# Retention, then a routed expert layer, then a squared-ReLU MLP: state products in four quarter tiles, first queries by blocks, later expert weights, other banks

## The chip, the cores and the metric

One Trainium2 core runs the whole program in one launch. The metric is the device time of one execution in microseconds. Before the change three executions took 484.52, 486.38 and 487.38 us; the median is 486.38 us.

## The reference

Three layers run one after the other, all in float32.

1. Retention. For each of 2 sequences and 8 heads (768 positions, head size 64), `state = gamma_h * state + outer(k_t, v_t)` and `y_t = q_t @ state / 8`. The heads' rows of 64 numbers side by side make 1536 tokens of 512 numbers.
2. Routed experts. `logits = x @ w_gate` for 8 experts; each token goes to its best expert, to the next free place there (384 places at most, in order of the tokens), through `relu(x @ w1[e]) @ w2[e]` (512 to 1024 to 512), and is scaled by its softmax weight. Tokens without a place give zero.
3. MLP: `relu(x @ w_in)**2 @ w_out`, 512 to 2048 to 512.

```python
state = gamma[None, :, None, None] * state + np.einsum('bhd,bhe->bhde', k[:, :, t], v[:, :, t])
y[:, :, t] = scale * np.einsum('bhd,bhde->bhe', q[:, :, t], state)
```

## The kernel before

Tokens are worked through in 12 tiles of 128 (6 for each sequence), the loop over `i` at L564, one turn for each tile. The order of every engine's queue is the order of the program, written out by hand (`manual_schedule`), so an instruction that waits holds up all behind it on its engine. TensorE is PE, VectorE DVE, ScalarE ACT, GpSimd POOL; SP issues nearly all DMAs.

Powers of gamma are folded into the rows of q and k: `khat` (L347, POOL) and `qhat` (L351, POOL) multiply, `ktrans` and `qtrans` (L360, L367) transpose four pairs of heads on PE and copy out of PSUM on ACT. Queries are loaded for two tiles at a time (L339, 512 KB). Tile `i` then needs three products. `scores` (L385) makes k times q for both heads of each of the 4 pairs, and DVE masks it into `A`. `outer` (L399) adds k times v to the running state in bank `pp`, and ACT copies it to `TF`. `attend` (L413) writes `xo`, transposed (features by tokens): the state's part at L423 (`TF` by the queries, float32, 64 rows by 64 columns of the array), then the part of the tile's own values at L426 (128 rows by 64 columns). At L423 head 0 of a pair uses rows 0 to 63 and columns 0 to 63, head 1 the other rows and the other columns, all into the one bank `xo`.

`halve` (L430) splits `xo` into two float16 halves, `xhi` on ACT and `xlo` on DVE. `gate` (L440) takes the logits from them in bank `lg`; `natural` (L471) transposes both back into bank `xn`, ACT copies them to `row`, and SP writes `row` to HBM. `probs`, `count`, `rank` (L497), `spread` and `enter` (L510) work out expert, weight and place; `rank` and `enter` use bank `lg` too. The eight PSUM banks are tk, tq, sc0, sc1, pp, xo, lg, xn, one tile in each.

Beside this the turns prepare the first expert's weights: 1 MB loads, their number capped by turn (L567), and splits into float16 halves, `split_hi` on ACT and `split_lo` on DVE (`half_step`, L268). From turn 3 on (`PRE`, L520) each turn has about one of each. The last two tiles are handled apart: turn 10 gathers the rows of expert 0 that are known (L582), runs `attend` of tile 11 inside the same turn (L598) and leaves the loop; L617 to L655 then add the last two tiles to expert 0's input through `p0` and the products into `xb` (L529, L634). The experts' layer starts behind it (L706) and PE is busy without a break from there to the end.

Of the kernel before, what the change touches and what calls it, by code (L numbers as in the profile page):

```python
# [27 lines left out]
def layout_consts(B, H, S, D, E, cap, widths):  # L28
# [9 lines left out]
    cols["gq"] = (gamma[None, None, :, None] ** (tq - S // 2) * 4.0).reshape(P, -1)  # L38
    cols["mask"] = (t[:, None] <= t[None, :]).astype(np.float64)
# [22 lines left out]
def kernel(  # L62
# [263 lines left out]

    Q, K, V = {}, {}, {}
# [3 lines left out]
    def load(i):  # L331
        b, c = divmod(i, NC)
        todo = [(K, k, "k")] + ([(Q, q, "q")] if c % 2 == 0 else []) + [(V, v, "v")]
        if i == 0:
            todo[0], todo[1] = todo[1], todo[0]
        for store, src, nm in todo:
            if store is Q:
                Q[i // 2] = ld.tile([P, H, 2, D], F32, name=nm, tag=nm, bufs=2)
                nc.sync.dma_start(Q[i // 2], src[b, :, c * P:(c + 2) * P, :].rearrange("h (p r) d -> p h r d", r=2))  # L339
            else:  # L340
                store[i] = ld.tile([P, H, D], F32, name=nm, tag=nm)
# [3 lines left out]
    HALF = [slice(j * D, (j + 1) * D) for j in range(2)]  # L345
# [5 lines left out]
    def qhat(u, r, eng=POOL):  # L351
        if 2 * u >= NT:
            return
        QH[u, r] = sb.tile([P, H, D], F32, name="qh", tag="qh")
        eng.tensor_tensor(QH[u, r], Q[u][:, :, r, :],
# [4 lines left out]
    def ktrans(i):  # L360
# [4 lines left out]
        ACT.activation(out=KT[i], in_=tk, func=AF.Copy)  # L365

    def qtrans(u, r, tag="tq", eng=ACT):  # L367
# [8 lines left out]
        o, x = QT[u][:, :, :, :, r], tq.rearrange("p n (c i) -> p n c i", c=2)  # L376
        if eng is DVE:
            DVE.tensor_copy(out=o, in_=x)
        else:
            ACT.activation(out=o, in_=x, func=AF.Copy)  # L380
# [32 lines left out]
    def attend(i):  # L413
        b, c = divmod(i, NC)
        xo = ps.tile([P, NP, P], F32, name="xo", tag="xo")
# [4 lines left out]
        if c:  # L420
            for p in range(NP):
                for r in HALF:
                    PE.matmul(xo[r, p, :], lhsT=TF[i][r, p, :], rhs=qt[r, p, :], start=(p == 0), stop=False, skip_group_check=True)  # L423
        for p in range(NP):
            for j, r in enumerate(HALF):
                PE.matmul(xo[r, p, :], lhsT=vv[:, 2 * p + j, :], rhs=a[:, j, p, :],  # L426
                          start=(c == 0 and p == 0), stop=(p == NP - 1), skip_group_check=True)
        XO[i] = xo

    def halve(i):  # L430
        xo = XO.pop(i)
# [39 lines left out]
    def natural(i, apart=False):  # L471
# [6 lines left out]
        if not apart:  # L478
            ACT.activation(out=row, in_=xn.rearrange("p s k t -> p s (k t)"), func=AF.Copy)
# [40 lines left out]
    PRE = 8  # L520
# [43 lines left out]
    for i in range(L):  # L564
        if i + LA < NT:
            load(i + LA)
        state["cap"] = min((i + 1) // 2 if i < 8 else i - 2, 4 * FIXED - 1)  # L567
        do_loads()
        if i == 5:
            clear()  # L570
# [44 lines left out]
        if L - PRE <= i and (i + 1) % NC:  # L615
            half_step(split_lo)
# [624 lines left out]
```

## Time and profile before

| | us |
|---|---|
| three executions | 484.52, 486.38, 487.38 |
| the profiled execution | 485.2 |
| its span, first to last instruction | 483.4 |
| attention's first product of tile 0's values (L426) | at 13.34 |
| experts' first product (L706) | at 87.15 |

An instruction's row gives its start, its duration, engine, line and the tiles it writes and reads; `x16` means that sixteen like it were merged. A float32 product on PE appears as two instructions. In brackets stands how long the engine idled before it, and for whom. A matmul's own duration (about 270 ns) overlaps with its neighbours'; what a group costs is the time from its start to the next group's start.

### The profile page before, as it was taken

How to read it: one execution, taken by the hardware profiler on the slowest of the kernel's cores; microseconds unless marked ns; L12 is line 12 of the kernel's file. 1: busy time of each engine (PE TensorE's matmuls, PEld its weight loads, DVE VectorE, ACT ScalarE, POOL GpSimd, SP SyncE). 2: the span in 40 equal slices, each digit the busy share in tenths (PEclk: the TensorE clock that was granted, in tenths of full speed). 3: DMA queues.
4: the chain of work that ended last, by engine and by line, in shares of the span. 5: the costliest groups of instructions: out<-in, count | busy, mean ns of one | idle time of the engine just before them, and what ended most of it. 6: DMA issues, size and time to landing. Idle time of an engine off the chain costs nothing.

```text
span 483.4 us, 10140 instructions
## 1 busy us (share of the span) xinstructions
PE 464.8 (96%) x4229; PEld 351.1 (73%) x4229; DVE 316.5 (65%) x552; ACT 265.3 (55%) x396; POOL 81.4 (17%) x99
## 2 busy tenths in 40 slices
PE   7999898999999999999999999999999999999994
PEld 4788787999999999999744444444458884447883
DVE  2457678898978879887699999407673114666111
ACT  2456666677667668663266666339882006885010
POOL 1544332542032131211200000020000110000001
PEclk8899999999999999999999999999999999999998
DMA  9999994799999979887443000011000100000001
GB/s 195 240 274 259 283 345 143 276 397 353 128 344 329 280 260 364 240 306 254 91 172 91 0 1 0 1 43 43 2 1 1 45 23 22 1 0 1 23 24 49
DMA packets 56120, 71.35 MB, mean 148 GB/s; under 512 B 30705, under 2 KB 37233, under 8 KB 55042
## 3 DMA queue, kind: packets, MB, share of 16 engines
q1 hardware_dynamic: 53410, 63.77, 43.9%
q0 software_dynamic: 2512, 6.73, 3.8%
q8 instruction: 35, 0.57, 0.5%
q10 hardware_dynamic: 144, 0.11, 0.2%
q14 instruction: 19, 0.16, 0.1%
HBM read 63.77 MB, written 6.84 MB: 146 GB/s over the span
## 4 chain that ended last, share of the span: by engine, by line
PE 81%; DVE 7%; DMA 4%; issue 3%; ACT 3%; POOL 1%; SPq 0%; POOLq 0%; ACTq 0%; DVEq 0%
PE w L1071 14%; PE zp L900 9%; PE zp L901 9%; PE zp L899 9%; PE yp L723 4%; PE yp L724 4%; PE yp L722 4%; PE hp L706 4%; PE hp L708 4%; PE hp L707 4%; PE op L925 3%; PE op L924 3%; PE op L923 3%; PE xo L426 2%; DMA gx<-xd,gidx 2%
## 5 line engine op out<-in xcount | busy, mean ns | idle before, releaser
L899 PE MATMUL zp<-yhi,winhi 128*128 128x512 f16 x192 | 72.8, 379 | 0.0
L901 PE MATMUL zp<-yhi,winlo 128*128 128x512 f16 x192 | 72.8, 379 | 0.0
L900 PE MATMUL zp<-ylo,winhi 128*128 128x512 f16 x192 | 72.8, 379 | 0.0
L723 PE MATMUL yp<-hl,w2hi 128*128 128x232 f16 (+5 forms) x256 | 65.5, 256 | 0.4 <-DVE hl L712 0.4
L722 PE MATMUL yp<-hh,w2hi 128*128 128x232 f16 (+5 forms) x256 | 65.5, 256 | 0.0
L724 PE MATMUL yp<-hh,w2lo 128*128 128x232 f16 (+5 forms) x256 | 65.5, 256 | 0.0
L1071 PE MATMUL w<-WH,AH 128*128 128x256 f16 x224 | 61.1, 273 | 0.5 <-ACT ob L1086 0.5
L1071 PE MATMUL w<-WL,AH 128*128 128x256 f16 x224 | 61.1, 273 | 0.0
L1071 PE MATMUL w<-WH,AL 128*128 128x256 f16 x224 | 61.1, 273 | 0.0
L706 PE MATMUL hp<-xg,w1hi 128*128 128x192 f16 (+5 forms) x224 | 57.1, 255 | 0.0
L708 PE MATMUL hp<-xg,w1lo 128*128 128x192 f16 (+5 forms) x224 | 57.1, 255 | 0.0
L707 PE MATMUL hp<-xg,w1hi 128*128 128x192 f16 (+5 forms) x224 | 57.0, 255 | 0.0
L914 POOL DMA_INDIRECT out_dram<-ob,tid x12 | 11.8, 982 | 224.2 <-DVE ob L1092 124.9
L1071 PEld LDWEIGHTS <-AH 128*128 128x128 f16 x448 | 43.8, 98 | 6.4 <-issue 0.9
L151 DVE SCALAR_TENSOR_TENSOR w2lo<-raw,w2hi 128x1024 f16<-128x1024 f32 x32 | 39.8, 1247 | 8.3 <-ACT w2hi L148 8.3
L1039 DVE TENSOR_TENSOR AL<-x,AH 128x768 f16<-128x768 f32 (+1 forms) x32 | 34.8, 1087 | 15.0 <-ACT AH L1037 15.0
L151 DVE SCALAR_TENSOR_TENSOR w1lo<-raw,w1hi 128x1024 f16<-128x1024 f32 x32 | 39.6, 1244 | 1.2 <-ACT w1hi L148 1.2
L900 PEld LDWEIGHTS <-winhi 128*128 128x128 f16 x192 | 18.8, 98 | 22.5 <-DVE ylo L729 0.2
L901 PEld LDWEIGHTS <-winlo 128*128 128x128 f16 x192 | 18.8, 98 | 22.6
L899 PEld LDWEIGHTS <-winhi 128*128 128x128 f16 x192 | 18.8, 98 | 22.5
L286 POOL DMA_INDIRECT gx<-xd,gidx x16 | 19.7, 1231 | 82.3 <-PE xt L689 72.3
L148 ACT ACTIVATE w2hi<-raw 128x1024 f16<-128x1024 f32 x32 | 33.4, 1051 | 0.0
(180 smaller groups left out, 995.7 us busy)
## 6 DMA issues: line engine op xcount, KB each, us to landing
raw<-in_moe_w_dram SPq DMA_DIRECT2D x32, 1024.0 KB, 7.3
rawi<-in_moe_w_in_dram SPq DMA_DIRECT2D x8, 1024.0 KB, 8.4
rawo<-in_moe_w_out_dram SPq DMA_DIRECT2D x8, 1024.0 KB, 7.0
q<-in_q_dram SPq DMA_DIRECT2D x6, 512.0 KB, 6.7
k<-in_k_dram SPq DMA_DIRECT2D x12, 256.0 KB, 4.5
v<-in_v_dram SPq DMA_DIRECT2D x12, 256.0 KB, 5.8
xd<-row SPq DMA_DIRECT2D x12, 256.0 KB, 4.0
xd<-zrow SPq DMA_DIRECT2D x2, 256.0 KB, 7.8
```

What stands on the lines that cost most here:

```text
L151: DVE.scalar_tensor_tensor(out=lo, in0=raw, scalar=WS, in1=hi, op0=ALU.mult, op1=ALU.subtract)
L706: PE.matmul(o, lhsT=w1h[:, kk, c], rhs=xh[kk], start=(kk == 0), stop=False)
L707: PE.matmul(o, lhsT=w1h[:, kk, c], rhs=xl[kk], start=False, stop=False)
L708: PE.matmul(o, lhsT=w1l[:, kk, c], rhs=xh[kk], start=False, stop=(kk == KD - 1))
L722: PE.matmul(o, lhsT=w2h[:, kk, c], rhs=hh[:, kk, :], start=(kk == 0), stop=False)
L723: PE.matmul(o, lhsT=w2h[:, kk, c], rhs=hl[:, kk, :], start=False, stop=False)
L724: PE.matmul(o, lhsT=w2l[:, kk, c], rhs=hh[:, kk, :], start=False, stop=(kk == KF - 1))
L899: PE.matmul(zp, lhsT=winhi[:, kk, c], rhs=yhi[kk // 2][:, kk % 2, cc], start=(kk == 0), stop=False)
L900: PE.matmul(zp, lhsT=winhi[:, kk, c], rhs=ylo[kk // 2][:, kk % 2, cc], start=False, stop=False)
L901: PE.matmul(zp, lhsT=winlo[:, kk, c], rhs=yhi[kk // 2][:, kk % 2, cc], start=False, stop=(kk == KD - 1))
L1039: DVE.tensor_tensor(AL[:, s, p, :], x[p][:, s, :], AH[:, s, p, :], op=ALU.subtract)
L1071: PE.matmul(o, lhsT=a[:, s, kk, c], rhs=b[:, kk, w, :], start=(start and n == 1), stop=(stop and n == end), skip_group_check=True)
```

## The change

- `attend` writes two PSUM tiles of half the size, `xo[0]` in bank `xo` (pairs 0 and 2) and `xo[1]` in bank `xn` (pairs 1 and 3). In the odd pairs the two heads change places in the output: rows 0 to 63 of the array go to columns 64 to 127, and the other way round. So the features of odd pairs lie swapped; `w_gate` is loaded with the same swap by four DMAs in place of one, `halve` works in two pieces, and `natural` swaps back with three ACT copies in place of one.
- The queries of tiles 0 and 1 are loaded as two blocks of 128 tokens (256 KB each), not as interleaved pairs; later query loads come one turn earlier. Buffers: q 3, k 3, v 5.
- The start is reordered: `khat(0)` and the copy of `ktrans(0)` go to DVE, `qhat(0, 1)` to POOL, and `scores(0)` stands before the second block's transposes.
- The loads of the experts' weights are capped lower in each turn, and the splits begin in turn 5 in place of 3. Turn 9 ends with two low splits in place of one, and turn 10 has one more high and low split, between `rank` and the end of the loop. By the experts' start the same nine have been made. The zeroing of the last rows moves from turn 5 to turn 7.
- `rank` uses bank `sc0` and `enter` bank `tk` for all but the last tiles, so `lg` holds logits alone.

```diff
     def later_consts():
         nc.sync.dma_start(c16, c16_d)
-        nc.sync.dma_start(wg, w_gate.rearrange("(k p) e -> p k e", p=P))
+        wgd = w_gate.rearrange("(k u j p) e -> u j p k e", u=2, j=2, p=D)
+        for u in range(2):
+            for j, r in enumerate(HALF):
+                nc.sync.dma_start(wg[r, u::2, :], wgd[u, j ^ u])
...
     def attend(i):
-        xo = ps.tile([P, NP, P], F32, name="xo", tag="xo")
+        xo = [ps.tile([P, NP // 2, P], F32, name="xo", tag=t) for t in ("xo", "xn")]
...
-                for r in HALF:
-                    PE.matmul(xo[r, p, :], lhsT=TF[i][r, p, :], rhs=qt[r, p, :], start=(p == 0), ...
+                for j, r in enumerate(HALF):
+                    PE.matmul(xo[p % 2][HALF[j ^ p % 2], p // 2, :], lhsT=TF[i][r, p, :], rhs=qt[r, p, :], start=(p < 2), ...
...
     def halve(i):
-        ACT.activation(out=xhi, in_=xo, func=AF.Copy, scale=XS)
-        DVE.scalar_tensor_tensor(out=xlo, in0=xo, scalar=XS, in1=xhi, op0=ALU.mult, op1=ALU.subtract)
+        for u, xo in enumerate(XO.pop(i)):
+            ACT.activation(out=xhi[:, u::2, :], in_=xo, func=AF.Copy, scale=XS)
+            DVE.scalar_tensor_tensor(out=xlo[:, u::2, :], in0=xo, scalar=XS, in1=xhi[:, u::2, :], op0=ALU.mult, op1=ALU.subtract)
...
     natural:
-            ACT.activation(out=row, in_=xn.rearrange("p s k t -> p s (k t)"), func=AF.Copy)
+            ACT.activation(out=o[:, :, :, 0], in_=x[:, :, :, 0], func=AF.Copy)
+            for j in range(2):
+                ACT.activation(out=o[:, :, :, 1, j], in_=x[:, :, :, 1, 1 - j], func=AF.Copy)
...
-        rk = ps.tile([P, E], F32, name="rk", tag="lg" if i < L - 1 else "pp")
+        rk = ps.tile([P, E], F32, name="rk", tag="sc0" if i < L - 1 else "pp")
-        tb_ = ps.tile([P, NB, E], F32, name="tb", tag="lg" if i < L - 1 else "pp" if i < L else "xn")
+        tb_ = ps.tile([P, NB, E], F32, name="tb", tag="tk" if i < L - 1 else "pp" if i < L else "xn")
...
-    PRE = 8
+    PRE = 6
...
-    qhat(0, 1, DVE)
-    khat(0, POOL)
+    khat(0, DVE)
     qtrans(0, 0)
-    qtrans(0, 1, "sc1", DVE)
-    ktrans(0)
+    ktrans(0, DVE)
+    qhat(0, 1, POOL)
+    scores(0)
     khat(1, POOL)
-    scores(0)
+    qtrans(0, 1)
+    outer(0)
     ktrans(1)
-    outer(0)
...
-        state["cap"] = min((i + 1) // 2 if i < 8 else i - 2, 4 * FIXED - 1)
+        state["cap"] = max(0, i - 1) // 2 if i < 8 else i - 3
-        if i == 5:
+        if i == 7:
             clear()
...
             attend(L)
             half_step(split_lo)
             rank(i)
+            half_step(split_hi)
+            half_step(split_lo)
             break
...
         if L - PRE <= i and (i + 1) % NC:
+            half_step(split_lo)
+        if i == L - 2:
+            half_step(split_hi)
             half_step(split_lo)
```

## Rows read from the trace of the kernel before

**Rows 1.** The page: busy time by engine, and PE in 40 slices of 12.1 us.
```profile
PE 464.8 (96%) x4229; PEld 351.1 (73%) x4229; DVE 316.5 (65%) x552; ACT 265.3 (55%) x396; POOL 81.4 (17%) x99
...
PE   7999898999999999999999999999999999999994
```

**Rows 2.** Busy time in four stretches: turns 1, 6, 7 and the tail.
```profile
20.35:26.48 6.13, 5.87 (x99) 5.21 (x97) 3.06 (x12) 2.79 (x7) 2.66 (x5) 1.00 0.99 221
...
51.17:57.41 6.24, 5.02 (x85) 4.36 (x82) 4.45 (x13) 4.16 (x10) 2.16 (x4) 1.00 1.02 326
57.41:63.60 6.19, 5.88 (x100) 5.21 (x98) 4.20 (x13) 4.16 (x10) 2.64 (x5) 1.00 1.00 250
...
80.16:87.15 6.99, 5.96 (x97) 5.33 (x96) 5.61 (x26) 4.80 (x10) 2.38 (x6) 1.00 0.42 129
```

**Rows 3.** The chain that ended last, in order of time, through turn 7.
```profile
57.48 1.02 PE xo L423 x16
58.50 1.05 PE xo L426 x16
...
59.63 0.61 ACT xhi L434
...
60.26 0.69 DVE xlo L435
60.95 0.10 DVE table L516
...
62.00 0.61 PE pp L408 x16
...
63.20 0.44 PE tq L375 x4
```

**Rows 4.** Waits in turns 0 to 10: total us, times, longest.
```profile
PE lg L444 <- DVE table L516: 2.8, 9, 0.3
...
PE rk L500 <- ACT pr L462: 1.6, 3, 0.9
```

**Rows 5.** Timeline of POOL in turns 0 and 1.
```profile
14.61 2.05 POOL L355 TENSOR_TENSOR qh<-q,c 128x512 f32<-128x512 f32 x2 [0.89 <-DMA q<-in_q_dram]
...
22.52 1.05 POOL L355 TENSOR_TENSOR qh<-q,c 128x512 f32<-128x512 f32 x1 [2.53 <-PE xo L426]
23.52 1.04 POOL L349 TENSOR_TENSOR kh<-k,c 128x512 f32<-128x512 f32 x1
```

**Rows 6.** Two stretches of the start: busy times, granted clock, DMA share, GB/s.
```profile
8.00:12.00 4.00, 3.31 (x23) 2.70 (x24) 0.80 (x2) 0.60 (x1) 1.04 (x1) 0.53 1.21 221
12.00:16.00 4.00, 4.00 (x49) 3.37 (x49) 1.06 (x4) 1.70 (x4) 2.44 (x3) 0.62 1.28 253
```

**Rows 7.** Timeline of turns 7 and 8: ACT copies and DVE splits.
```profile
57.13 0.37 ACT L411 ACTIVATE tf<-pp 128x256 f32<-128x256 f32 x1
...
57.95 1.22 DVE L151 SCALAR_TENSOR_TENSOR w1lo<-raw,w1hi 128x1024 f16<-128x1024 f32 x1
...
62.08 1.02 ACT L479 ACTIVATE row<-xn 128x1024 f16<-128x1024 f16 x1 [0.92 <-ACT w2hi L148]
...
64.41 2.06 DVE L151 SCALAR_TENSOR_TENSOR w2lo<-raw,w2hi 128x1024 f16<-128x1024 f32 x1
```

**Rows 8.** Timeline of the tail.
```profile
80.16 1.09 PE L423 MATMUL xo<-qt,tf 64*64 64x128 f32 x16
80.32 1.02 ACT L479 ACTIVATE row<-xn 128x1024 f16<-128x1024 f16 x1 [0.64 <-ACT w2hi L148]
...
82.73 0.34 DVE L526 TENSOR_SCALAR p<-c,rnk,oh 128x232 f16<-128x232 f16 x1
...
83.12 0.95 PE L532 MATMUL xb<-p,row 128*128 128x232 f16 x8 [0.70 <-DVE p L526]
```

**Rows 9.** SP's issue of the gate's weights, in the timeline.
```profile
7.82 0.43 SPq L310 DMA_DIRECT2D wg<-in_moe_w_gate_dram  x1
```

**Rows 10.** The page: the weights' loads, KB each, us from issue to landing.
```profile
raw<-in_moe_w_dram SPq DMA_DIRECT2D x32, 1024.0 KB, 7.3
```

More of the change, by code (lines that the diff above doesn't have):

```diff
@@ L325 @@
     R = [cst.tile([P, E], F16, name=f"R{i}") for i in range(2)]
+    HALF = [slice(j * D, (j + 1) * D) for j in range(2)]
     Q, K, V = {}, {}, {}
@@ L332, in load @@
         b, c = divmod(i, NC)
-        todo = [(K, k, "k")] + ([(Q, q, "q")] if c % 2 == 0 else []) + [(V, v, "v")]
-        if i == 0:
-            todo[0], todo[1] = todo[1], todo[0]
+        u = i // 2 if i in (2, 4) else (i + 1) // 2 if i > 4 and i % 2 else NT
+        todo = [(K, k, "k")] + ([(Q, q, "q")] if 2 * u < NT else []) + [(V, v, "v")]
+        if i < 2:
+            todo = [(Q, q, "q"), (K, k, "k"), (V, v, "v")]
         for store, src, nm in todo:
-            if store is Q:
-                Q[i // 2] = ld.tile([P, H, 2, D], F32, name=nm, tag=nm, bufs=2)
-                nc.sync.dma_start(Q[i // 2], src[b, :, c * P:(c + 2) * P, :].rearrange("h (p r) d -> p h r d", r=2))
+            if store is Q and i < 2:
+                if i == 0:
+                    both = ld.tile([P, 2, H, D], F32, name=nm, tag=nm, bufs=3)
+                    Q[0, 0], Q[0, 1] = both[:, 0], both[:, 1]
+                nc.sync.dma_start(Q[0, i], src[b, :, c * P:(c + 1) * P, :].rearrange("h t d -> t h d"))
+            elif store is Q:
+                Q[u] = ld.tile([P, H, 2, D], F32, name=nm, tag=nm, bufs=3)
+                bq, cq = divmod(2 * u, NC)
+                nc.sync.dma_start(Q[u], src[bq, :, cq * P:(cq + 2) * P, :].rearrange("h (p r) d -> p h r d", r=2))
             else:
-                store[i] = ld.tile([P, H, D], F32, name=nm, tag=nm)
+                store[i] = ld.tile([P, H, D], F32, name=nm, tag=nm, bufs=3 if store is K else 5)
                 nc.sync.dma_start(store[i], src[b, :, c * P:(c + 1) * P, :].rearrange("h t d -> t h d"))
     QH, KH, KT, QT, A = {}, {}, {}, {}, {}
-    HALF = [slice(j * D, (j + 1) * D) for j in range(2)]
     def khat(i, eng=POOL):
@@ L358, in qhat, with ktrans @@
             Q.pop(u)
-    def ktrans(i):
+    def ktrans(i, eng=ACT):
         tk = ps.tile([P, NP, P], F32, name="tk", tag="tk")
@@ L364, in ktrans @@
         KT[i] = sb.tile([P, NP, P], F32, name="kt", tag="kt")
-        ACT.activation(out=KT[i], in_=tk, func=AF.Copy)
+        if eng is DVE:
+            DVE.tensor_copy(out=KT[i], in_=tk)
+        else:
+            ACT.activation(out=KT[i], in_=tk, func=AF.Copy)
     def qtrans(u, r, tag="tq", eng=ACT):
@@ L376, in qtrans @@
         o, x = QT[u][:, :, :, :, r], tq.rearrange("p n (c i) -> p n c i", c=2)
+        if u == 0:
+            o, x = QT[u][:, :, r].rearrange("p n i r -> p n (i r)"), tq
         if eng is DVE:
@@ L421, in attend @@
             for p in range(NP):
-                for r in HALF:
-                    PE.matmul(xo[r, p, :], lhsT=TF[i][r, p, :], rhs=qt[r, p, :], start=(p == 0), stop=False, skip_group_check=True)
+                for j, r in enumerate(HALF):
+                    PE.matmul(xo[p % 2][HALF[j ^ p % 2], p // 2, :], lhsT=TF[i][r, p, :], rhs=qt[r, p, :], start=(p < 2), stop=False,
+                              skip_group_check=True)
         for p in range(NP):
-            for j, r in enumerate(HALF):
-                PE.matmul(xo[r, p, :], lhsT=vv[:, 2 * p + j, :], rhs=a[:, j, p, :],
-                          start=(c == 0 and p == 0), stop=(p == NP - 1), skip_group_check=True)
+            for j in range(2):
+                PE.matmul(xo[p % 2][HALF[j ^ p % 2], p // 2, :], lhsT=vv[:, 2 * p + j, :], rhs=a[:, j, p, :],
+                          start=(c == 0 and p < 2), stop=(p >= NP - 2), skip_group_check=True)
         XO[i] = xo
     def halve(i):
-        xo = XO.pop(i)
         xhi = sb.tile([P, KD, P], F16, name="xhi", tag="xhi")
         xlo = sb.tile([P, KD, P], F16, name="xlo", tag="xlo")
-        ACT.activation(out=xhi, in_=xo, func=AF.Copy, scale=XS)
-        DVE.scalar_tensor_tensor(out=xlo, in0=xo, scalar=XS, in1=xhi, op0=ALU.mult, op1=ALU.subtract)
+        for u, xo in enumerate(XO.pop(i)):
+            ACT.activation(out=xhi[:, u::2, :], in_=xo, func=AF.Copy, scale=XS)
+            DVE.scalar_tensor_tensor(out=xlo[:, u::2, :], in0=xo, scalar=XS, in1=xhi[:, u::2, :], op0=ALU.mult, op1=ALU.subtract)
         XT[i] = (xhi, xlo)
@@ L478, in natural @@
         if not apart:
-            ACT.activation(out=row, in_=xn.rearrange("p s k t -> p s (k t)"), func=AF.Copy)
+            o, x = [y.rearrange("p s (k u) (j d) -> p s k u j d", u=2, j=2) for y in (row.rearrange("p s (k t) -> p s k t", k=KD), xn)]
+            ACT.activation(out=o[:, :, :, 0], in_=x[:, :, :, 0], func=AF.Copy)
+            for j in range(2):
+                ACT.activation(out=o[:, :, :, 1, j], in_=x[:, :, :, 1, 1 - j], func=AF.Copy)
         else:
```

5 lines of the change are left out of this document (added).

## Prediction

> **What bounds the kernel now.** I read the page first: PE is busy for 96% of the span, and the slices show where it is not: in the first seven, the attention [rows 1]. From the experts' first product at 87.15 us to the end PE has no break, and the change touches nothing there, so its whole worth is how much earlier that product starts. The stretches by turn come next: turns 1 to 9 take 6.12 to 6.24 us each, with PE busy for 5.9 of it in turns 1 and 7 and 5.0 in turn 6, and the other engines well below [rows 2]. So a turn is PE's. The chain through turn 7 shows what PE does and where it waits: the state's part 1.02, the values' part 1.05, then ACT's xhi 0.61, DVE's xlo 0.69 and table 0.10 [rows 3]; the scores run on PE beside those three, and when they are through PE still waits for the table before it can write logits, 0.3 us in each of 9 turns [rows 4]. In three turns it waits up to 0.9 for the softmax to leave the same bank [rows 4]. Turns 0 and 1 are different: there POOL waits for queries that have not landed [rows 5] while the DMA engines are full (share 1.2 to 1.3, 221 to 253 GB/s) [rows 6].
>
> The sum is made against the profiled execution: 485.2 us, a span of 483.4 and 1.8 around it. It lies 1.2 below the median of the three runs, 486.4; the gain is taken off both.
>
> **The state's part.** Sixteen instructions take 1.02 us, 64 ns each; a full-array transpose with the same 128 moving columns takes 0.44/4 = 0.11 us [rows 3]. So two quarter tiles run side by side, eight steps of 0.11 with some fill. The change gives four quarters in turn. The array's halves work side by side by rows in the scores and by columns in the values' part (1.05 for sixteen) [rows 3]; four at once no row shows. Bounds: four steps, 0.44 less each tile; no gain; or one at a time, 16 x 0.11 = 1.76, 0.74 more than now. I take four steps, nearest to what each pair of neighbours does already.
>
> The trace has two row halves writing different partitions of one bank at the same time, since all of L423 goes to bank `xo` [rows 3]. The Trainium skill, TensorEngine Tiling (Array Packing), section Restrictions and Gotchas, says that different row tiles cannot access the same PSUM bank simultaneously. By that rule only two of the four could run at once, one in each bank, and this term would be nothing. The row speaks against the rule for separate partitions; it is a rival below.
>
> The values' part has the same instructions; two neighbours now share a column half, and I leave it at 1.05 (up to 0.2 more if the queue looks ahead too little; less than now is excluded, since both halves are full today).
>
> **Other banks, and halving in two pieces.** With table and ranks out of `lg` the logits wait for xhi and xlo alone. A piece of xhi costs 0.37, as a copy of 128x256 does [rows 7]; a piece of xlo is 0.42 by estimate (0.69 for 512 columns [rows 3], less half the columns at 1.05 ns). The first piece is complete two products before the second. So xlo ends about 1.0 after the values' part, not 1.4, while the scores hold PE until 1.3: hidden, and the 0.3 us wait goes. What is late next is DVE's argmax for the rank; it comes 3.3 after the values' part, and PE reaches the rank at 3.7.
>
> The row in three ACT copies costs about 0.60 + 0.37 + 0.37 less overlap, 1.2 where 1.02 stands [rows 7]. The values' next tile now waits for it, as `xn` is shared. Within a turn the copies end 3.5 after the values' part and the next state's part starts at 3.8: hidden, by 0.3. Without that cover it would be 0.3 a turn.
>
> A full turn is then 6.19 - 0.31 - 0.44 = 5.44. Turns 2, 3, 5, 7 and 8 gain 0.75 each, 3.75. Turn 4, without outer products, also loses a wait for the softmax: 1.05. Turn 6 has no state's part; its rank waits for the argmax and no longer for the softmax: 0.8. Turn 9: 0.9. Tile 10's state part 0.44. Together 6.9.
>
> Against it stands DVE. A low split takes 1.22, or 2.06 where POOL works beside it [rows 7]. In a turn of 5.44 it starts 4.2 after the values' part, and the next xlo wants DVE at 5.65; 1.22 fits, 2.06 makes the logits 0.5 late. POOL's two products fall on the splits of turns 6 and 7: -0.6. Middle: **+6.3**.
>
> **The start.** Less has to land before the first transposes, and tile 0 comes some 2 us earlier. But the bytes ahead of the next queries stay the same, so POOL's products at 14.61 and 22.52 stand where they were [rows 5]. The second row names PE, whose part ended 0.05 before; the engine needs nothing of PE there, so I take it for the landing of the queries. `khat(3)` queues behind it on POOL and ends at 24.56, and tile 3's transposes wait for it. Then transposes of 0.5 and 0.44 and the rank: tile 2's products start at 25.7, against 26.48 now: **+0.8**. The gate's weights as four DMAs add 3 x 0.43 = 1.3 us on SP's queue [rows 9] ahead of these loads; SP runs ahead of the full DMA engines, so I price it at nothing, at worst -1.3. If the queries land 1.2 earlier the gain is 2.0. K with three buffers waits for nothing, since `khat` of the buffer's last user is two turns old.
>
> The weights' loads cost nothing: the first is wanted in turn 5 and issued in turn 3, 10.9 us ahead, with 7.3 to land [rows 10]. At worst one ACT split waits behind, with the row copy queued after it, for 1 us. The zeroing has three turns to land: nothing, at worst some tenths behind the row writes.
>
> **The tail.** Three things lie on the path to the experts. Turn 9's second low split needs its high split, which stands on ACT behind kt; DVE is through 1.4 us too late for tile 10's xlo. Tile 11's products follow tile 10's transposes at once (80.16, while the row is copied from 80.32 [rows 8]); its odd pairs now wait 1.2 for the three copies, less 0.44 for the state's part: 0.8. And the added low split stands on DVE between the rank and `p0`, for which PE already waits 0.70 at 83.12 [rows 8]: 1.2. With the last row's extra copies 0.1: **-3.5** (bounds -2 if the first two overlap, -5 if splits take 2.06).
>
> **Sum.** 0.8 + 6.3 - 3.5 = 3.6 us. 485.2 - 3.6 = 481.6 for the profiled execution; against the median 486.4 - 3.6 = **482.8**.
>
> **Rivals.**
> (a) The clock falls in the new gaps. PE would idle some 2.8 us in turn 1 (21.8 to 24.6) and 4 to 5 us in pieces in the tail. In the start of before, after PE had waited for q and k, the granted clock was 0.53 and 0.62 over 8 us, that is the lower level, 1.2 GHz, for most of it [rows 6]. One such spell of 3.4 to 6.8 us loses 1.7 to 3.4: 484.5 to 486.2. For it: the gaps are as long as those ahead of the fall. Against: in the tail before, 85% busy, the clock stayed at 1.00 [rows 2].
> (b) Two quarters at a time: nine tiles give back 0.44, 486.7.
> (c) Slower: DVE becomes the bound of turns 6 to 11. If POOL's work falls on every split, seven of them lie on the path at 2.06 in place of 1.22: 5.9, of which 0.6 is counted, so 488.1, and with a spell of the lower clock behind the longer tail 489.8. It decides once a split in a turn takes over 1.5. For it: one of the splits shown is at 2.06 [rows 7]. Against: POOL has no product left for turns 9 and 10.
> (d) One quarter at a time: the ten tiles lose 1.18 each against the forecast, 494.6. Today's 64 ns speaks against it [rows 3].
> (e) Better: queries earlier (+1.2) and the delays of the tail overlapping (+1.5): 480.1.
>
> **Chances.** Forecast 0.38, own range 481.3 to 484.3; (a) 0.22, (b) 0.10, (c) 0.10, (d) 0.05, (e) 0.15. A measurement of this kernel can tell 0.5% from no change, 2.4 us. Faster by more: 0.30 of the forecast, all of (e), 0.03 of (a): 0.48. Slower: (d), 0.08 of (c), 0.02 of (b): 0.15. The rest, 0.37, is within. The range of 479.6 to 487.6 leaves out (d), most of (c) and the fast end of (e).
>
> **What would show it.** Right: sixteen L423 in about 0.57 us; no wait of lg for the table; turns 2, 3 and 5 near 5.45; POOL's second qh near 22.5 and tile 2's products near 25.7; L532 waiting about 2 us for `p0`; the experts' first product near 83.5. Wrong: L423 still at 1.02; a granted clock of 0.5 after 20 us; splits of 2.06 in most late turns; or queries landing with the earlier start, which would make turns 0 and 1 shorter than 6 us.

## The result, and the profile after

The changed kernel takes **489.22 us** (median of 10, 486.53 to 491.5) beside 485.41 for the kernel before on the same chip (10, 484.52 to 487.59): ratio 1.0073, 95% interval 1.0052 to 1.0095. I had forecast 482.8, 3.6 us faster; it is 3.5 us slower by the ratio, 3.8 between the medians. The profiled execution took 489.91 us, a span of 488.1 and 1.8 around it; the one of before had a span of 483.4. These two single executions lie 4.7 apart.

The page of the changed kernel, busy time, PE's slices and its granted clock, beside [rows 1]:

```profile
PE 464.0 (95%) x4229; PEld 348.7 (71%) x4229; DVE 320.8 (66%) x564; ACT 268.9 (55%) x432; POOL 80.7 (17%) x99
...
PE   7899996899999999999999999999999999999993
...
PEclk8899999899999999999999999999999999999997
```

PE is busy for as long as before (464.0 for 464.8) in a longer span. The seventh slice, 73 to 85 us, has a 6 where before had an 8: the loss is in the tail of the attention. The stretches, as in [rows 2] (turn 1, turn 7, tail to the experts' first product; busy PE, PEld, DVE, ACT and POOL, then clock, DMA share, GB/s):

```profile
21.48:27.45 5.97, 5.53 (x100) 4.76 (x98) 3.22 (x13) 3.37 (x10) 2.94 (x5) 0.99 1.17 290
54.26:60.71 6.45, 5.77 (x99) 5.01 (x97) 5.84 (x14) 4.75 (x14) 2.64 (x6) 1.00 0.81 210
77.31:90.03 12.72, 7.98 (x98) 6.61 (x97) 6.78 (x28) 6.38 (x16) 3.43 (x6) 0.73 0.49 163
```

Turn 1 is 0.16 shorter than before, turn 7 is longer (6.45 for 6.19), and the tail takes 12.7 us at a mean clock of 0.73, where before took 7.0 at 1.00. Laid out by stretch, both profiled executions (first products of each tile), with the gain that the prediction's terms give for each:

| stretch | before | changed | gain predicted | gain measured |
|---|---|---|---|---|
| start to tile 2 | 26.48 | 27.45 | +0.8 | -1.0 |
| turns 2 to 6 | 30.93 | 26.81 | +4.1 | +4.1 |
| turns 7 to 9 | 18.50 | 17.72 | +1.8 | +0.8 |
| tile 10 to the first product with `p0` | 7.21 | 10.34 | -3.0 | -3.1 |
| from there to the experts' first product | 4.03 | 7.71 | -0.1 | -3.7 |
| experts to the end of the span | 396.3 | 398.1 | 0 | -1.8 |
| sum | 483.4 | 488.1 | +3.6 | -4.7 |

**Turns 2 to 6.** The timeline of PE in turn 3, beside L423 and L426 in [rows 3]:

```profile
32.84 0.67 PE L447 MATMUL xo<-qt,tf 64*64 64x128 f32 x16
33.44 1.09 PE L451 MATMUL xo<-A,v 128*64 128x128 f32 x16
```

From the first of the sixteen to the values' part it is 0.60 us instead of 1.02, and the values' part is as long as it was. PE's waits over the whole span, beside [rows 4]: the line for the table is gone, and others head the list.

```profile
PE tq L395 <- POOL qh L372: 2.3, 1, 2.3
PE xb L667 <- DMA gx<-xd,gidx: 2.0, 2, 1.3
PE xb L560 <- DVE p L554: 1.8, 1, 1.8
PE lg L472 <- DVE xlo L460: 1.3, 4, 0.6
...
PE xo L447 <- ACT row L507: 0.9, 1, 0.9
```

**The start.** SP's issues in the timeline, beside [rows 9], and then two of these microseconds in the view of [rows 6]:

```profile
8.19 2.66 SPq L316 DMA_DIRECT2D wg<-in_moe_w_gate_dram  x4
10.90 0.59 SPq L317 DMA_DIRECT2D c32t<-in_c_dram  x1
11.54 0.43 SPq L357 DMA_DIRECT2D k<-in_k_dram  x1
12.01 0.58 SPq L354 DMA_DIRECT2D q<-in_q_dram  x1
```

```profile
10.50:12.50 2.00, 2.00 (x24) 1.47 (x23) 1.12 (x2) 0.98 (x2) 0.37 (x1) 0.78 0.24 33
```

The same two microseconds in the kernel before:

```profile
10.50:12.50 2.00, 2.00 (x16) 1.45 (x16) 1.01 (x2) 0.00 (x0) 0.00 (x0) 0.50 1.17 239
```

The four loads of the gate's weights hold SP for 2.66 us in place of 0.43. The next keys are issued at 11.54 (8.85 before), and the DMA engines run dry: 33 GB/s at a share of 0.24, where before had 239 at 1.17. POOL, beside [rows 5], starts the queries at 17.43 and 24.29 instead of 14.61 and 22.52:

```profile
14.96 1.04 POOL L363 TENSOR_TENSOR kh<-k,c 128x512 f32<-128x512 f32 x1 [4.09 <-DMA k<-in_k_dram]
17.43 2.06 POOL L372 TENSOR_TENSOR qh<-q,c 128x512 f32<-128x512 f32 x2 [1.43 <-DMA q<-in_q_dram]
...
24.29 1.05 POOL L372 TENSOR_TENSOR qh<-q,c 128x512 f32<-128x512 f32 x1 [3.34 <-DMA q<-in_q_dram]
```

**Turns 7 and 8.** DVE's low splits of turns 6 and 7, beside the last of [rows 7], and POOL's products at the same time:

```profile
55.64 2.06 DVE L153 SCALAR_TENSOR_TENSOR w1lo<-raw,w1hi 128x1024 f16<-128x1024 f32 x1
...
61.83 2.06 DVE L153 SCALAR_TENSOR_TENSOR w1lo<-raw,w1hi 128x1024 f16<-128x1024 f32 x1
```

```profile
54.55 1.05 POOL L372 TENSOR_TENSOR qh<-q,c 128x512 f32<-128x512 f32 x1
55.56 1.05 POOL L363 TENSOR_TENSOR kh<-k,c 128x512 f32<-128x512 f32 x1
...
60.74 1.05 POOL L372 TENSOR_TENSOR qh<-q,c 128x512 f32<-128x512 f32 x1
61.75 1.06 POOL L363 TENSOR_TENSOR kh<-k,c 128x512 f32<-128x512 f32 x1
```

**The tail.** The timeline of all engines, beside [rows 8]:

```profile
78.66 0.65 PE L447 MATMUL xo<-qt,tf 64*64 64x128 f32 x12 [0.92 <-ACT row L507]
...
80.60 1.22 DVE L153 SCALAR_TENSOR_TENSOR w2lo<-raw,w2hi 128x1024 f16<-128x1024 f32 x1
...
81.08 1.77 POOL L288 DMA_INDIRECT gx<-xd,gidx  x1 [8.36 <-DVE junk L532]
...
81.93 0.34 DVE L554 TENSOR_SCALAR p<-c,rnk,oh 128x232 f16<-128x232 f16 x1
...
82.32 1.02 PE L560 MATMUL xb<-p,row 128*128 128x232 f16 x8 [1.84 <-DVE p L554]
...
83.15 0.94 POOL L288 DMA_INDIRECT gx<-xd,gidx  x1 [0.30 <-DVE xlo L460]
...
85.97 0.29 PE L667 MATMUL xb<-c,gx 128*128 128x128 f16 x1 [1.33 <-DMA gx<-xd,gidx]
...
86.91 1.62 PE L667 MATMUL xb<-c,gx 104*128 104x104 f16 x15 [0.65 <-DMA gx<-xd,gidx]
...
88.48 1.63 PE L560 MATMUL xb<-p,row 128*128 128x232 f16 x8
...
90.03 0.26 PE L739 MATMUL hp<-xghi,w1hi 128*128 128x232 f16 x1
```

Up to `p0` it is close to the forecast: PE waits 0.92 for the row copies, and 1.84 for `p0` behind the added low split. One wait ahead of it was not in the sum. In turn 9 ACT's row copy waits until an earlier row's write has landed (row 7's, issued at 62.31 and landed at 71.21), and tile 10's turn is 5.33 us, where the version with the gate's weights on ACT's queue, without this wait, has 4.92:

```profile
71.31 0.60 ACT L505 ACTIVATE row<-xn 128x512 f16<-128x512 f16 x1 [1.22 <-DMA xd<-row]
```

What follows `p0` was not in the sum either. The gather of expert 0's rows is issued at 81.08 and 83.15 (79.07 and 80.53 before), though its numbers were in `gidx0` at 75.97; PE waits 1.33 and 0.65 for it, and sixteen gathered products and the eight products of the last `p0` take 1.62 and 1.63 where before they took 1.01 and 0.95. The granted clock is down meanwhile, 0.57 over this stretch:

```profile
82.00:90.00 8.00, 5.70 (x60) 4.99 (x60) 3.07 (x17) 2.33 (x7) 2.50 (x6) 0.57 0.47 138
```

The row names DVE as what POOL waited for (8.36 us), but DVE had long been done. By the trace's semaphore events POOL's wait ended at 80.25, on the semaphore that the write of row 9 raises, the last row that the gather must find in memory. That write was issued at 72.49, so the gather waited for it until 7.8 us later; a row's write with little beside it, the tail's, lands in 2.0. In the kernel before the same write landed 2.6 us after its issue.

### The profile page after: what moved, and what is told of

The parts are those of the page before. It is cut to its first block, busy times and chain, and to the rows that moved or that the text cites. A ratio compares the mean times of both kernels' runs of the same rounds, so it can differ in the third digit from the quotient of the medians.

```text
span 488.1 us, 10222 instructions
## 1 busy us (share of the span) xinstructions
PE 464.0 (95%) x4229; PEld 348.7 (71%) x4229; DVE 320.8 (66%) x564; ACT 268.9 (55%) x432; POOL 80.7 (17%) x99
## 4 chain that ended last, share of the span: by engine, by line
PE 77%; DMA 7%; DVE 6%; issue 3%; POOL 2%; SPq 2%; ACT 2%; POOLq 0%; ACTq 0%; DVEq 0%
PE w L1104 14%; PE zp L934 8%; PE zp L932 8%; PE zp L933 8%; PE yp L756 4%; PE yp L757 4%; PE yp L755 3%; PE hp L741 3%; PE hp L739 3%; PE hp L740 3%; PE op L958 3%; PE op L956 3%; PE op L957 3%; DMA gx<-xd,gidx 3%; DMA q<-in_q_dram 2%
```

## The experiments

My theory after this reading: the change's own terms are about right, and three costs that the sum did not hold turn it round: (1) the four loads on SP's queue, (2) weights' loads that stand before row 9's write on the DMA engines, (3) the clock, which falls in the tail's gaps. The rivals: the bytes set the landings in any order, and the quarters bring nothing. Ratios are to the kernel before on the same chip, all with 6 to 12 executions.

### Gate's weights on ACT's queue

```diff
-    nc.sync.dma_start(wg[r, u::2, :], wgd[u, j ^ u])      # in later_consts
+    nc.scalar.dma_start(wg[r, u::2, :], wgd[u, j ^ u])    # ahead of the warm-up products
```

> The changed kernel with one edit: the four loads of the gate's weights are issued from ACT's queue instead of SP's. Theory A (SP's queue starves the start): tile 2's keys are issued at about 8.8 us instead of 11.5, the DMA engines never run dry between 10.5 and 13, POOL's kh of tile 2 starts near 12.5 (14.96 in the changed kernel), tile 2's products start near 25 (27.45), and the total falls by 2.5 to 4 us to 485 to 487 us. Rival B (the bytes set the landing, not the issue, as my prediction had it): tile 2's products stay within 0.5 us of 27.45 and the total within 0.7 us of the changed kernel's 489.2.

Measured: 486.36 us, ratio 1.0025 (1.0003 to 1.0047), that is 2.3 us of the loss back. The next keys are issued at 8.78, and POOL:

```profile
12.99 1.04 POOL L358 TENSOR_TENSOR kh<-k,c 128x512 f32<-128x512 f32 x1 [2.00 <-DMA k<-in_k_dram]
14.93 2.06 POOL L367 TENSOR_TENSOR qh<-q,c 128x512 f32<-128x512 f32 x2 [0.89 <-DMA q<-in_q_dram]
...
22.57 1.05 POOL L367 TENSOR_TENSOR qh<-q,c 128x512 f32<-128x512 f32 x1 [4.13 <-PE pp L425]
```

Tile 2's products start at 25.73; the prediction said 25.7. Theory A. The profiled executions of all runs on the changed kernel bear it out: with the four loads on SP's queue tile 2's products start at 27.45 to 28.88 us (four executions), with the loads on ACT's at 25.45 to 26.03 (nine), on average 2.4 us earlier, as much as the total gains. In the tail the gather is still late (76.32 and 78.82), though row 9's write now lands in 5.2 us, and the clock still falls.

### Weights' loads as before

```diff
-        state["cap"] = max(0, i - 1) // 2 if i < 8 else i - 3
+        state["cap"] = min((i + 1) // 2 if i < 8 else i - 2, 4 * FIXED - 1)
-        if i == 7:
+        if i == 5:
             clear()
```

> The changed kernel with one edit: the raw loads of the experts' weights and the zeroing of the last rows are issued in the turns of the kernel before (first load in turn 1, zeroing in turn 5). Theory A (late weights sit ahead of row 9's write on the DMA rings, and POOL's gather waits for that write): the write of row 9 lands within 4 us of its issue instead of 7.8, the gather is issued before 79 us instead of 81.1, PE's 2.0 us of waiting for gathered rows is gone, and the total falls by 2 to 3.5 us to 485.7 to 487.2. Rival B (the bytes only move: early weights delay the queries, keys and values of turns 2 to 5 by as much): turns 2 to 6 become longer by 2 us or more together and the total stays within 0.7 us of 489.2.

Measured: 488.91, ratio 1.0091 (1.0061 to 1.0121): no gain. The last load was issued 5 us ahead of row 9's write, which still takes 7.0 us to land, and the gather is no earlier:

```profile
80.82 1.15 POOL L288 DMA_INDIRECT gx<-xd,gidx  x1 [7.24 <-DVE w2lo L153]
```

So it is not the turn in which the weights are issued. The engines ran at 403 to 410 GB/s from 68 to 76 us: the same bytes now have to pass in fewer microseconds of attention. Theory A's cure fails; whether its culprit is right, two later runs tell (held weights, and the weights' part alone).

### Weights' loads and splits as before

```diff
-    PRE = 6
+    PRE = 8
...
-            half_step(split_hi)
-            half_step(split_lo)
```

Both added pairs of half steps go, and the loads are those of the run before this one.

> The kernel of the run with early weights, and also the splits where the kernel before has them (from turn 3 on, none added in turns 9 and 10). Theory A (the added splits delay xlo of tile 10 and the first places p0 of the tail): tile 10's turn, 5.33 us, falls to about 4.0, p0 comes 1.1 us earlier after the rank, and the total is 1.5 to 2.5 us below the run with early weights, 483.5 to 485.5. Rival B (the tail waits for the row copies, the logits' chain and the gather in any case): within 0.7 us of the run with early weights.

Measured: 489.56, ratio 1.0110 (1.0073 to 1.0148). The tail does get shorter: tile 10's turn 3.73 instead of 4.91, and PE waits 0.80 for `p0`, not 1.84. But the two early splits fall beside POOL's products in turns 4 and 5 (2.06 us each), and these turns take 5.86 and 6.45 instead of 5.07 and 5.41. What the tail gains the middle gives back: rival B in the total, by another way.

### Fillers in the tail's gaps

```diff
+    for j in range(7):       # ahead of p0's products; 12 more, into bank xo, ahead of the gathered rows
+        PE.matmul(xb[0][0].rearrange("p a b -> p (a b)"), lhsT=warm[:, 0:P], rhs=warm, start=True, stop=True)
```

> The changed kernel with 19 products of 512 columns on zeros added in the tail, 7 while PE waits for p0 and 12 while it waits for the gathered rows; their results are never read. Theory A (the gaps of the tail cost twice, once as waits and once because the clock falls to 0.5 behind them): the granted clock stays at 1.0 between 75 and 95 us, the experts' first product starts 1.5 to 2 us earlier than 90.0, and the total falls to 487 to 488. Rival B (the clock's fall costs nothing, because DVE, the gather and the weights' splits set the start of the experts): the clock stays up but the first product stays within 0.4 us of 90.0, or comes later by the fillers that still run when the rows land, and the total stays at 489 or above.

Measured: 488.12, ratio 1.0062 (1.0040 to 1.0085), 0.5 us better than the changed kernel, which the two intervals leave open. The clock stayed at 1.00 from 75 to 95 us (0.83 in the changed kernel), but the twelve fillers ran on until 88.54, after the rows had come, and the experts' first product comes at 90.50, no earlier than 90.03. For the time this is inconclusive; the clock stayed up where the gaps were filled, in this one execution.

### Weights held until row 9 is written

```diff
-        state["cap"] = max(0, i - 1) // 2 if i < 8 else i - 3
+        state["cap"] = min(max(0, i - 1) // 2 if i < 8 else i - 3, 4 if i < L - 1 else 6)
```

On top of the gate's weights on ACT's queue.

> The run with the gate's weights on ACT's queue, and one more edit: no raw load beyond expert 0's four (the first four) is issued before row 9's write; two more follow it in turn 10, the rest after the tail. Theory A (row 9's write stands behind megabytes of weights on the rings, and the gather waits for it): the write lands within 4 us of its issue (7.8 in the changed kernel), the gather is issued before 75.5 us on that run's clock (76.3 and 78.8 there), PE waits for no gathered row, 16 gathered products follow the rank at once, and the total falls by 1.5 to 3 us to 483.4 to 484.9. Rival B (the DMA engines have so many bytes to move that the gather lands at the same time in any order): within 0.7 us of that run's 486.4. Rival C (the held weights are missed later): the experts start earlier, but the first products of experts 0 and 1 then wait for weights and the total does not fall.

Measured: 484.67, ratio 0.9987 (0.9962 to 1.0012), 1.8 us better than without (the intervals leave 0.2 to 3.5). The row's write, in the view of DMA issues, lands after 4.0 us, 5.2 in the run that this one starts from:

```profile
xd<-row SPq DMA_DIRECT2D x1, 256.0 KB, 4.0
```

The gather is issued at 76.76 and 78.20, 4.88 us behind tile 10's first product instead of 6.05, PE waits for no gathered row (0.6 there), and the last DVE step of the experts comes 1.9 us earlier than in the kernel before: the held weights are not missed. Theory A; the held weights had been in the way.

### Row 9's write on ACT's queue

```diff
-        nc.sync.dma_start(xd[1 + i * P:1 + (i + 1) * P], row)
+        (nc.scalar if i == L - 2 else nc.sync).dma_start(xd[1 + i * P:1 + (i + 1) * P], row)
```

With the gate's weights on ACT's queue and all loads where the change has them.

> The run with the gate's weights on ACT's queue, and one more edit: row 9's write alone is issued from ACT's queue, with all loads where the changed kernel has them. If the write is late because it stands behind the weights in SP's own queue (theory A1), it now lands within 4 us of its issue, and the gather and the total go as with held loads: 1.5 to 3 us less than 486.4. If it is late because the DMA engines are full and share themselves among the queues (theory A2), it still takes 6 us or more, and the total stays within 0.7 us of 486.4.

Measured: 487.32, ratio 1.0057 (1.0037 to 1.0077). The write has a queue of its own and still takes

```profile
xd<-row ACTq DMA_DIRECT2D x1, 256.0 KB, 6.6
```

That is no less than the 5.2 on SP's queue: A2. With the engines full, being first in a queue did not help; only fewer bytes did. The total says less, since the edit cost something of its own: ACT's next row copy now waits 2.7 us until this write has landed, PE waits 2.1 for the copies instead of 0.9, and the run is 1.6 us slower than the one it starts from.

### Held weights and fillers ahead of `p0`

```diff
+    for j in range(7):      # ahead of p0's products; none ahead of the gathered rows
+        PE.matmul(xb[0][0].rearrange("p a b -> p (a b)"), lhsT=warm[:, 0:P], rhs=warm, start=True, stop=True)
```

> The run with held loads, and 7 products of 512 columns on zeros while PE waits for p0, never read. Theory A (the idle time ahead of p0 still lets the clock fall by itself): with held loads alone the granted clock is 0.5 for one spell of about 3.4 us or more between 80 and 88 us, here it stays at 1.0, and the experts' first product comes 1 us or more earlier. Rival B (once the gather's wait is gone the tail is busy enough): the clock is 1.0 in both, and the total is within 0.7 us of held loads alone.

Measured: 482.95, ratio 0.9962 (0.9944 to 0.9979): faster than the kernel before. Against held weights alone it is 1.2 us, and the two intervals overlap. In the profiled execution of held weights alone the clock happened to stay up in the tail, so that pair doesn't show it; without fillers it fell between 77 and 92 us in six of the seven profiled executions that have the gap ahead of `p0` (the changed kernel and five others), with them in one of five, and there ahead of the fillers. That the clock falls in these gaps is shown; that it costs 1.2 us of the median is not.

### Pairs side by side in another order

```diff
-            for p in range(NP):
+            for p in (*range(0, NP, 2), *range(1, NP, 2)):
```

> The run with held loads, with one edit: the state's part is issued even pairs first, odd pairs behind, so that neighbours use the same two quarters of the array and only two run side by side. All else, banks, pieces and copies, stays. Theory A (four quarters at a time are worth 0.44 us in each of ten tiles, as the prediction had it): the sixteen take about 1.0 us from first to last start instead of 0.45, turns 2 to 6 are 0.4 to 0.5 longer each, and the total is 3.5 to 4.6 us above held loads alone. Rival B (the quarters only move the waiting: POOL, DVE and the landings set the turn): the turns stay at 5.4 us and the total within 1 us.

Measured: 484.25, ratio 0.9976 (0.9952 to 1.0000), the same as held weights alone, and the state's part in turn 3 too:

```profile
30.86 0.68 PE L442 MATMUL xo<-qt,tf 64*64 64x128 f32 x16
31.47 1.09 PE L446 MATMUL xo<-A,v 128*64 128x128 f32 x16
```

Neither theory: the edit did not undo the quarters. By their starts in the trace, the first products of the other two quarters begin 27 ns behind those of the first two, though a second pair for the first two stands between, and from then on each quarter goes through its own. The order hardly matters; a later experiment undoes the quarters properly.

### The kernel before with the four loads

```diff
-        nc.sync.dma_start(wg, w_gate.rearrange("(k p) e -> p k e", p=P))
+        wgd = w_gate.rearrange("(k u j p) e -> u j p k e", u=2, j=2, p=D)
+        for u in range(2):
+            for j, r in enumerate(HALF):
+                nc.sync.dma_start(wg[r, u::2, :], wgd[u, j])
```

> The kernel before with one edit: the gate's weights come in four loads on SP's queue, as in the changed kernel, in place of one (same bytes, same place in the queue). Theory A (each of the four holds SP for 0.6 us and the DMA engines run dry behind them): tile 2's keys are issued near 10.6 us instead of 8.85, POOL's kh of tile 2 starts near 14.3 (12.68 before), the first qh of pair 1 near 16.2 (14.61), tile 2's products near 27.7 to 28 (26.48), and the total rises by 1 to 1.8 us to 486.4 to 487.2. Rival B (SP runs ahead of full engines, as the prediction had it): tile 2's products within 0.4 us of 26.5 and the total within 0.7 us of 485.4.

Measured: 487.57, ratio 1.0050 (1.0029 to 1.0072), 2.4 us slower. POOL starts the keys and queries at

```profile
14.39 1.04 POOL L352 TENSOR_TENSOR kh<-k,c 128x512 f32<-128x512 f32 x1 [4.03 <-DMA k<-in_k_dram]
16.79 2.05 POOL L358 TENSOR_TENSOR qh<-q,c 128x512 f32<-128x512 f32 x2 [1.35 <-PE xn L479]
```

Theory A in the total, from the other side: three more DMAs of the same bytes, 0.5% of the kernel, more than the 1 to 1.8 us expected. Where the time goes this one trace shows only in part: tile 2's products come 0.5 us later than before (26.98, not 27.7 to 28) and the experts' first product 1.0 later.

### The kernel before with the weights' part

```diff
-        state["cap"] = min((i + 1) // 2 if i < 8 else i - 2, 4 * FIXED - 1)
+        state["cap"] = max(0, i - 1) // 2 if i < 8 else i - 3
-    PRE = 8
+    PRE = 6
...
```

With `clear()` in turn 7 and the two added pairs of half steps.

> The kernel before with the weights' part of the change alone: raw loads and zeroing in the later turns, splits from turn 5 on, and the added splits in turns 9 and 10. Theory A (this part costs by itself, whatever the turns' length: the added splits delay tile 10 and p0, and row 9's write stands behind weights): tile 10's turn grows from 4.25 to 5 us or more, p0 comes at least 1 us later after the rank, the gather 0.5 to 1.5 us later, and the total rises by 1.5 to 3 us to 487 to 488.5. Rival B (it costs only where the turns are faster than the loads, so not here): the total within 0.8 us of 485.4.

Measured: 486.99, ratio 1.0027 (1.0006 to 1.0049): slower by 1.3, a little less than theory A said. PE waits 2.05 for `p0` (0.70 before), row 9's write takes 4.4 us to land (2.6 before, 3.8 in the run above), the gather is issued 0.5 later although tile 2 started 1.4 earlier in this execution, and the clock falls in the tail; tile 10's turn is 4.50, not 5.

### Fillers in the start

```diff
+        if i < 2:
+            wu1 = ps.tile([P, 512], F32, name="wu1", tag="tk")
+            for j in range((4, 6)[i]):
+                PE.matmul(wu1, lhsT=warm[:, 0:P], rhs=warm, start=True, stop=True)
```

> The run with held loads and fillers in the tail (482.95 us), and 4 + 6 more products on zeros while PE waits for the next queries in turn 0 and for the next keys in turn 1, never read. Theory A (the waits of the start let the clock fall in many executions, at 17 us or at 26 us, each fall costing up to 1.5 us): no granted clock of 0.5 between 12 and 470 us, and the median falls by 0.5 to 1.2 us with less spread. Rival B (the landing of the queries hides the slower clock): within 0.4 us of 482.95.

Measured: 484.47, ratio 0.9971 (0.9951 to 0.9991). The clock stayed at 1.00 from 6 to 477 us, and the time is no better than without: rival B. Tile 2's products start at 25.81, inside the 25.45 to 26.03 of the other versions with this start, some of which have the lower clock for a part of it: there the landing of the queries covers the slower clock.

### Two quarters instead of four

```diff
-                    PE.matmul(xo[p % 2][HALF[j ^ p % 2], p // 2, :], lhsT=TF[i][r, p, :], rhs=qt[r, p, :], start=(p < 2), stop=False,
+                    PE.matmul(xo[p % 2][HALF[j], p // 2, :], lhsT=TF[i][r, p, :], rhs=qt[r, p, :], start=(p < 2), stop=False,
```

The values' part, the gate's weights and the odd row copies follow in the same way; the rest is the run with held weights and fillers ahead of `p0`.

> The run with held loads and fillers in the tail (482.95 us), with the quarters alone undone: each head's products go to the half of the array that its rows have, so that only two of the four quarters are used, as before; the two banks, the pieces and the three copies stay. (Pairs issued side by side in another order still gave 0.61 us, as the engine issues an instruction every 7 ns and each quarter works through its own.) Theory A: the sixteen take 1.0 us again, turns 2 to 6 are 0.4 to 0.45 longer each, and the total is 3 to 4.4 us higher, 486 to 487.4. Rival B (two banks, not four quarters, made the sixteen faster): still 0.6 us and within 0.7 us of 482.95.

Measured: 485.71, ratio 0.9997 (0.9979 to 1.0016), 0.35% above the run it starts from, 1.7 us (intervals leave 0.4 to 3). The state's part in turn 3:

```profile
31.52 1.09 PE L442 MATMUL xo<-qt,tf 64*64 64x128 f32 x16
32.54 1.10 PE L446 MATMUL xo<-A,v 128*64 128x128 f32 x16
```

1.02 us again; turns 2 to 5 and 9 are 0.42 longer each (5.82 for 5.40). Theory A for the mechanism, with less in the total than the 3 to 4.4 I gave: turns 7 and 8 stay at 6.45 and 6.19, because there DVE sets the time.

### POOL's products ahead of the split

```diff
         if i >= 1:
             enter(i - 1)
+        if 5 <= i < L - 1:
+            qhat(*turn(i + 1))
+            if i + 3 < NT:
+                khat(i + 3)
```

With the same two calls behind the rank only for i < 5.

> The run with held loads and fillers in the tail (482.95 us, ratio 0.9962 to before), with POOL's products for the next queries and keys issued at the head of turns 5 to 9 instead of behind the rank, so that they run beside DVE's xlo and A, not beside the split. Theory A (DVE's low split takes 2.06 instead of 1.22 and its table of places 0.86 instead of 0.31 only because POOL works at the same time, and that is what lengthens turns 7 and 8): the splits of turns 6 to 8 take 1.2 us, turns 7 and 8 fall from 6.46 and 6.19 to 5.4 to 5.6, and the total falls by 1.2 to 1.8 us to 481.2 to 481.8. Rival B (the delay only moves: xlo and A become longer by as much, or the logits wait for ACT): turns 7 and 8 stay above 5.9 and the total within 0.6 us.

Measured: 482.42, ratio 0.9939 (0.9919 to 0.9959). DVE's splits of turns 6 and 7:

```profile
53.98 1.21 DVE L153 SCALAR_TENSOR_TENSOR w1lo<-raw,w1hi 128x1024 f16<-128x1024 f32 x1
...
58.90 1.22 DVE L153 SCALAR_TENSOR_TENSOR w1lo<-raw,w1hi 128x1024 f16<-128x1024 f32 x1
```

Turns 7 and 8 fall from 6.46 and 6.19 to 5.75 and 5.40, theory A for the turns; in turn 7 the keys land late. In the total it is less than the 1.2 to 1.8 us of the theory: tile 10's turn grows from 5.01 to 5.79, since ACT's row copy in turn 9 waits 1.05 for the write of row 7, so part of the delay moves after all. The gain against the run without the edit (0.2%) lies within the two intervals; the rows carry the verdict on the splits. The Trainium skill, "SBUF — State Buffer", section "SBUF: two separate sides", says that a DVE instruction with two inputs from SBUF and a GpSimd one that reads there lock each other out of a pair of ports for a whole instruction; by that rule a split waits for the product in front of it, and the trace agrees, with 2.06 us beside POOL and 1.21 alone.

### The pair of splits behind `p0`

```diff
             rank(i)
-            half_step(split_hi)
-            half_step(split_lo)
             break
...
     spread(L - 1)
+    half_step(split_hi)
+    half_step(split_lo)
     half_step(split_hi)
```

With POOL's products early, without fillers.

> The run with early POOL products, without fillers, and with the pair of splits that stands between the rank of tile 10 and p0 moved behind p0 and tile 11's xlo. Theory A (the added low split delays p0 by its own 1.2 us, as the prediction had it, and the gap ahead of p0 is what lets the clock fall): p0's products start within 0.8 us of the rank instead of 1.8 to 2.0, the clock stays at 1.0 through the tail without fillers, and the total is 0.3 to 1 us below the run with early POOL products. Rival B (DVE's chain of tile 11 then waits for the split instead): p0 is earlier, but tile 11's logits or their argmax come as late as before, and the total is the same within 0.5 us or higher, since the gap has only moved.

Measured: 481.98, ratio 0.9945 (0.9923 to 0.9968): the same as with fillers. PE's waits for `p0` and for tile 11's argmax:

```profile
78.17 0.95 PE L555 MATMUL xb<-p,row 128*128 128x232 f16 x8 [0.70 <-DVE p L549]
...
80.81 0.17 PE L523 MATMUL rk<-OH,c 128*128 128x8 f16 x1 [0.93 <-DVE nb L476]
```

0.70 instead of 1.84, and the clock stayed at 1.00 with no filler; theory A for the place. Of the gain half moves on: tile 11's rank now waits 0.93 for DVE instead of 0.33, and the total is rival B's.

## Why the prediction was wrong

**The start** failed at the step "SP runs ahead of the full DMA engines, so I price it at nothing, at worst -1.3". SP's lead was too short. When the four issues begin, at 8.19, the engines are full (225 GB/s from 8 to 9 us), but they run dry at 10.5; the four issues take 2.66 us, and the next keys go out only at 11.54 (33 GB/s in between). The term was +0.8 and came out at -1.0; adding the four loads alone costs 2.4 us and taking them off SP gives back 2.3. Without them the rest of the step holds: tile 2 at 25.73, 25.7 forecast. I had also taken the duration from [rows 9], one load, for each of the four.

**The weights' loads** failed at "The weights' loads cost nothing". I asked when each load is wanted and how long it takes to land, and not what stands behind it on the same engines. Row 9's write did, and the gather behind that, and the experts behind the gather. Holding back three loads gives 1.8 us. From `p0` to the experts' first product the seven versions with held weights take 4.1 to 5.0 us, the six on the changed kernel without 5.3 to 7.7, and the kernel before 4.0. Earlier loads (488.91) and a queue of the write's own (487.32) give nothing, since it is the bytes in flight, 400 GB/s up to 78 us. In the kernel before the same bytes had 4 us more of attention to pass in. The write's landing points to that: 2.6 to 4.4 us in the three versions with turns as slow as before, whichever the turn of the loads, and 5.2 to 7.7 in the six with faster turns and nothing held, again whichever the turn of the loads. So it is the faster turns, more than the loads' place in them, that the sum had to reckon with. In the table's stretch behind `p0` (-3.7 for -0.1) the waits for gathered rows are 2.0, the largest single part; the clock adds 1.3.

**The clock**: rival (a) was right that the granted clock falls to the lower level, 1.2 GHz, in the tail's gaps, in most profiled executions; my argument against it, that the tail of before stayed at 1.00, was no argument, since that tail had no gap of 1.8 us (0.70 at `p0`). Its price in the changed kernel is some 1.3 us by estimate: 24 products took 3.25 us instead of 1.96. As a rival it was priced by itself; it came on top of the gather.

**The middle** was right in mechanism and, for turns 2 to 6, in size: 4.1 forecast, 4.1 measured. The state's part lost 0.42 (0.44 forecast), the wait for the table is gone, the row's three copies are hidden. Rivals (b) and (d) fall. On the rule of the Trainium skill that the prediction weighed (TensorEngine Tiling (Array Packing), section Restrictions and Gotchas: row tiles not in the same PSUM bank at the same time), the trace decides against it for separate partitions: two row tiles share bank `xo` and two share `xn`, and four run together, 0.60 us for sixteen. In turns 7 to 9 the term for DVE was mis-sized: 0.6 for two splits at 2.06, and 1.6 measured (2.4 without it by the forecast, 0.8 found). The sum had left out that POOL's products also delay the instruction ahead of the split, the table of places in `spread` (1.14 and 0.87 us ahead of these two splits, 0.32 without POOL), and in turns of 5.4 us nothing covers that. That is rival (c)'s mechanism in two turns; moving POOL's products gives most of it back in these turns. That the measured time lies between the 488.1 and 489.8 of rival (c) is chance: it had seven splits on the path.

**The tail to `p0`**: -3.0 forecast, -3.1 measured; the row copies cost 0.92, the added low split 1.22 ahead of `p0`. The mechanism is right and the size nearly so: some 0.4 of the 3.1 is the late write of row 7, and without it the stretch is 2.7 to 2.8 longer than before (9.93 and 9.99 in two versions, 7.21 before), so part of that fit is luck.

**After the experts' start** I had zero and it was -1.8. Of this 0.85 is waiting for later gathers and for DVE between 90 and 230 us: the stretch up to the first product of the final layers takes 149.8 us, 148.9 before and 148.2 to 149.1 in the versions with held weights. The other 1.0 lies behind DVE's last step of the first token block of the final layers, where nothing differs; that stretch takes between 172.3 and 173.7 us over the profiled executions of all versions, so I don't put it down to the change. Its cause stays open.

With the gate's weights off SP's queue, three loads held, the gap ahead of `p0` filled and POOL's order changed, the kernel takes 0.9939 of the time before (0.9919 to 0.9959), 3.0 us less: close to the 3.6 that I had forecast for the change without these edits. It beats both kernels.

## What to carry to other kernels

Before a step is called hidden, count what it does to the queue and the engines that it shares, not only when its own result is wanted: a DMA issue holds its queue (0.4 to 0.7 us each here), and megabytes of prefetch delay the small write that a gather waits for (2.6 us became 5 to 8). When a middle gets faster, ask which transfers lose the time in which they used to pass. A stall that is added in front of TensorE may cost twice, once as a wait and once as the lower clock behind it.

## What the runs showed of the hardware

- Four loads of 128 elements of 32 bytes hold SP 2.66 us, one load of the same 512 elements 0.43: three more DMAs cost 2.2 us of the queue for no more bytes.
- A 256 KB write that lands in 2.0 us with little beside it took 5.2 to 7.7 behind weights on its own queue and 6.6 on another queue, with the engines at 400 GB/s.
- Products for two idle quarters of TensorE started 27 ns behind the first, ahead of products for busy quarters that stand before them in the program: two orders of the same sixteen gave 0.60 and 0.61 us.
- Beside a POOL product of 1.05 us a split on DVE took 2.06 instead of 1.21 us.
